# Queries and keys handed over with the head dimensions first: the on-chip transposes and copies ahead of the feature projection go away

## The chip, the core and the metric

The kernel runs on one core of a Trainium2 chip. The metric is device time in microseconds (us), from launch to the last output in memory; how the host arranges its arrays before the launch is not in it. Five engines work side by side, each through its own instructions in order: TensorE (PE: matrix products and transposes; its weight loads have their own row, PEld), VectorE (DVE), ScalarE (ACT), GpSimd (POOL) and SyncE (SP, which here only issues DMAs). Products land in PSUM, everything else lies in SBUF.

## What is computed

Three stages follow each other, for 4 batches of 576 tokens with 8 heads of 64 dimensions (2304 tokens of 512 features). Cut to what matters:

```python
def phi(x):                                   # (b, h, s, 64) -> (b, h, s, 256)
    proj = einsum('bhsd,df->bhsf', x, w_phi)  # 64 -> 128 features
    proj = proj - max(abs(proj), axis=-1)
    return concatenate([exp(proj), exp(-proj)])
q_p, k_p = phi(q), phi(k)
kv = einsum('bhsf,bhsd->bhfd', k_p, v);  z = sum(k_p, axis=2)
x = (q_p @ kv) / (q_p . z + 1e-6)             # linear attention
# experts: each token goes to its best of 8 (512 -> 1024 relu -> 512), scaled by two gates
# last: RMS norm, silu(xn @ w_gate) * (xn @ w_val) @ w_out, 512 -> 1536 -> 512
```

## The kernel before

**Staging.** Attention, gating and experts of all four batches come first, planned together; the last stage comes after a branch (lines 978 and 979) that all engines reach. Attention of batch b (`attn`, line 376) goes over nine groups of [128 tokens x 4 chunks x 2 heads]: four pairs of heads of k over the first 512 tokens, one group "L" with the 64 left-over tokens of all heads (k and q together), four pairs of q.

**One group.** `load` brings 256 KB into a `qk` tile (4 of them), tokens on the partitions. `proj` (line 411) then needs the 64 head dimensions on the partitions, since a product sums over them: four 128x128 transposes on PE into a PSUM bank `pa` (line 418), one ACT copy to an SBUF tile `x0` (line 421), eight products with `w_phi` (line 428; each stands as two records in the trace) into a double bank `pp` (named pq in the trace), the largest magnitude on DVE (432), and the subtraction on DVE (434), which frees `pp`. Exponentials on ACT follow (522, 515, or 451 after transposes for q), then the products with v (492), the key sums (478 to 501), the transposes of kv (539), and for q the products 589, the division (459 to 463), transposes, and the halves of `xh`, the experts' input (600, 602).

**Experts.** The experts of batch b (lines 737 and 746, twelve 128x288 products per task) need all of its `xh`. They have a lower priority than attention and fill PE while the attention of later batches goes on.

**What sets the order.** `Graph` is a planner that runs while the kernel is built. It gives every task an assumed duration, starts whichever can start first on each engine, then the one of lower priority number, and so writes down a fixed order for each engine. Buffers of a tag come from slots; a task without a free slot waits. `retire` (lines 314 and 315) takes one `pp` double bank from attention after nine uses of `pp`, and one `pa` bank after a count of uses, and hands them to the experts as `ph` banks. So from the tenth projection on, there is one `pp`.

Of the kernel before, what the change touches and what calls it, by code (L numbers as in the profile page):

```python
# [13 lines left out]
ALU = mybir.AluOpType  # L14
# [3 lines left out]
B, H, S, D = 4, 8, 576, 64  # L18
FE = 128
# [10 lines left out]
class Buf:  # L30


    def __init__(self, tag, ap=None, hold=False):
        self.tag, self.ap, self.hold = tag, ap, hold
        self.writers, self.all, self.left, self.end, self.slot = [], [], 0, 0.0, None
# [189 lines left out]
def act(n, psum=True):  # L225
    return 0.15 + n / 1200.0


class K:
    def __init__(self, tc, q, k, v, w_phi, wg, wo, w1, w2, mg, mv, mo, rg, out):  # L230
        self.tc, self.nc = tc, tc.nc
        self.q, self.k, self.v, self.w_phi = q, k, v, w_phi
        self.wg, self.wo, self.w1, self.w2 = wg, wo, w1, w2
        self.mg, self.mv, self.mo = (a.bitcast(U32) for a in (mg, mv, mo))
        self.rg, self.out = rg, out
        self.g = Graph()
        self.marks = []
# [64 lines left out]
    def psum(self):  # L302


        self.banks, self.pair = ExitStack(), ExitStack()
        p = self.pool(self.banks, "ps", space=PSUM)
        one = [p.tile([P, 512], F32, name=f"ps{i}") for i in range(4)]
        two = [p.tile([P, 2, 512], F32, name="pq0"),
               self.pool(self.pair, "pq", space=PSUM).tile([P, 2, 512], F32, name="pq1")]
        self.last = two[0]  # L310
        self.g.slot("pa", one)
        self.g.slot("pp", two)
        self.g.slot("ph", [])
        self.g.retire("pp", 9, two[1], "ph", self.halve)
        self.g.retire("pa", 36, one[3], "ph", lambda: one[3:])

    def halve(self):

# [32 lines left out]
    def attn_slots(self, ctx):  # L351
        g, p = self.g, self.pool(ctx, "at", side="left")
        self.attn_consts(p)
        mk = lambda *a: self.mk(p, *a)
        mk("qk", 4, [P, 2, NC, D])
        mk("v", 3, [P, 2, NC, D])
        mk("vl", 2, [P, 2, NC, D])
        mk("x0", 2, [P, NC, P])
        mk("d", 3, [P, 2, NC, FE])
        mk("m", 3, [P, 2 * NC])  # L360
        mk("e", 2, [P, 2 * NC, 2, FE])
        mk("el", 1, [P, NC, 2, FE])
        for _, _, a in g.slots["vl"]:
            self.nc.gpsimd.memset(a, 0.0)
        self.ones = p.tile([P, 1], F32, name="ones")
        self.nc.gpsimd.memset(self.ones, 1.0)
        mk("es", 2, [P, 4, 2 * FE])
        mk("ks", 1, [P, 2 * FE])
        mk("qp", 2, [P, 2, NC, P])
        mk("qpl", 1, [P, 2, NC, P])  # L370
        mk("kv", 6, [P, 2, 2, D + 1])
        mk("x", 2, [P, NC, P])
        mk("xl", 1, [P, 4 * D])
        mk("r", 2, [P, NC])

    def attn(self, b, prio):
# [6 lines left out]
        def load(src, pr, np_):  # L383
            t = g.buf("qk")
            if pr != "L":
                g.t("SP", 0.5, lambda: nc.sync.dma_start(
                    t.ap, src[b, 2 * pr:2 * pr + 2, 0:MAIN].rearrange("h (p c) d -> p h c d", c=NC)),
                    w=[t], prio=np_, nbytes=2 * MAIN * D * 4)
                return t
            for i, m in enumerate((self.k, self.q)):  # L390
                for j in range(2):
                    g.t(eng, 0.6, lambda i=i, j=j, m=m: dma(
                        t.ap[j * 64:(j + 1) * 64, i], m[b, j::2, MAIN:S].rearrange("h t d -> t h d")),
                        w=[t], prio=-1 if b == 0 else np_, nbytes=LEFT * H * D * 2)
            return t

        def load_v(pr, np_):
# [12 lines left out]

        def proj(t, np_):

            pt, xt, m, d, pp = (g.buf(n) for n in ("pa", "x0", "m", "d", "pp"))

            def tr():
                for j in range(2):
                    for c in range(2):
                        nc.tensor.transpose(pt.ap[:, (2 * j + c) * P:(2 * j + c + 1) * P],
                                            t.ap[:, j, 2 * c:2 * c + 2].rearrange("p a d -> p (a d)"), self.ident)
            g.t("PE", 4 * 0.109, tr, r=[t], w=[pt], prio=np_)  # L420
            g.t("ACT", act(512), lambda: nc.scalar.copy(  # L421
                xt.ap.rearrange("p c t -> p (c t)"), pt.ap), r=[pt], w=[xt], prio=np_)

            def mm():
                for k in range(NC):
                    for hf in range(2):
                        r = slice(hf * 64, hf * 64 + 64)
                        nc.tensor.matmul(pp.ap[:, hf, k * FE:(k + 1) * FE], lhsT=xt.ap[r, k], rhs=self.wraw[r],  # L428
                                         start=True, stop=True)
            g.t("PE", 8 * 0.109 + 0.2, mm, r=[xt, self.cBw], w=[pp], prio=np_)  # L430
            pv = lambda: pp.ap.rearrange("p h (k f) -> p (h k) f", f=FE)
            g.t("DVE", dve(1024), lambda: nc.vector.tensor_reduce(  # L432
                out=m.ap, in_=pv(), axis=AX.X, op=ALU.max, apply_absolute_value=True), r=[pp], w=[m], prio=np_)
            g.t("DVE", dve(1024), lambda: nc.vector.tensor_tensor(  # L434
                out=d.ap.rearrange("p h k f -> p (h k) f"), in0=pv(),
                in1=m.ap.unsqueeze(2).to_broadcast([P, 2 * NC, FE]), op=ALU.subtract),
                r=[m, pp], w=[d], prio=np_)
            return d

        at = lambda j, c: (c % 2) * NC + 2 * j + c // 2  # L440

        def queries(d, j, qp, np_):

            pd = g.buf("pa")

            def tr():
                return [partial(nc.tensor.transpose, pd.ap[:, c * P:(c + 1) * P], d.ap[:, c % 2, 2 * j + c // 2],
                                self.ident) for c in range(NC)]
            g.t("PE", NC * 0.109, tr, r=[d], w=[pd], prio=np_, kind="pass", steps=NC)
            for f in range(2):  # L450
                g.t("ACT", act(512), lambda f=f: nc.scalar.activation(  # L451
                    qp.ap[:, f].rearrange("p c t -> p (c t)"), pd.ap, AF.Exp, scale=1.0 - 2.0 * f),
                    r=[pd], w=[qp], prio=np_)
            return pd
# [15 lines left out]
        def kv_part(pr, e, v, np_, pk, part, pz=None):  # L470
# [1 line left out]

            es = g.buf("es") if NC in part else None
            if es:
                ev = lambda: e.ap.rearrange("p (a k) f x -> p a k (f x)", a=2)
                sv = lambda: es.ap.rearrange("p (j b) x -> p j b x", j=2)
                ex = lambda: el.ap[:, (pr % 2) * 2 + pr // 2].rearrange("p f x -> p (f x)")
                g.t("DVE", dve(1024), lambda: nc.vector.tensor_tensor(
                    out=es.ap, in0=ev()[:, 0], in1=ev()[:, 1], op=ALU.add), r=[e], w=[es], prio=np_)
                g.t("DVE", dve(512), lambda: nc.vector.tensor_tensor(  # L480
                    out=sv()[:, :, 0], in0=sv()[:, :, 0], in1=sv()[:, :, 1], op=ALU.add), rw=[es], prio=np_)
                for j in range(2):
                    r = slice(j * 64, j * 64 + 64)
                    g.t("DVE", dve(256), lambda j=j, r=r: nc.vector.tensor_tensor(
                        out=sv()[r, j, 0], in0=sv()[r, j, 0], in1=ex()[r], op=ALU.add), r=[el], rw=[es], prio=np_)

            def fn():
                for c in part:
                    for j in range(2):
                        v_, e_ = (v.ap[:, j, c], e.ap[:, at(j, c)]) if c < NC else (  # L490
                            vl.ap[:, j, pr], el.ap[:, (pr % 2) * 2 + pr // 2])
                        nc.tensor.matmul(pk.ap[j * 64:j * 64 + 64, 0:2 * FE], lhsT=v_,
                                         rhs=e_.rearrange("p f e -> p (f e)"), start=(c == 0), stop=(c == NC))
# [13 lines left out]
        for i, pr in enumerate([0, "L", 1, 2, 3]):  # L507
# [4 lines left out]
            if pr == "L":  # L512
                el, vl, qpl = g.buf("el"), v, g.buf("qpl")
                for f in range(2):
                    g.t("ACT", act(512, False), lambda f=f, d=d: nc.scalar.activation(
                        el.ap[:, :, f].rearrange("p (h c) f -> p h c f", h=2), d.ap[:, :, 0:2], AF.Exp,
                        scale=1.0 - 2.0 * f), r=[d], w=[el], prio=np_)
                queries(d, 1, qpl, np_)
            else:
                e = g.buf("e")  # L520
                for f in range(2):
# [54 lines left out]
        for pr in range(NC):  # L576
# [3 lines left out]
            x = g.buf("x")  # L580
            for j in range(2):
                qp = g.buf("qp")
                pn = queries(d, j, qp, np_ + j)

                def nm(pn=pn, qp=qp, pr=pr, j=j):
                    for c in range(NC):
# [452 lines left out]
    return UT if u < B else B * LEFT  # L1039


def build(tc, ctx, q, k, v, w_phi, wg, wo, w1, w2, mg, mv, mo, rg, out):
    kk = K(tc, q, k, v, w_phi, wg, wo, w1, w2, mg, mv, mo, rg, out)
    nc, g = tc.nc, kk.g
    kk.consts(ctx)
    kk.psum()
# [56 lines left out]
    with tc.manual_schedule():  # L1103
# [10 lines left out]
        g.emit()  # L1114


_INS = ["q", "k", "v", "w_phi", "moe_w_gate", "moe_w_output_gate", "moe_w1", "moe_w2",
        "moe2_w_gate", "moe2_w_val", "moe2_w_out", "moe2_rms_g"]


# [19 lines left out]
```

## Time and profile before

| | us |
|---|---|
| runs, median (lowest to highest) | 871.34 (870.13 to 871.94) |
| the profiled execution | 868.49 |
| its span, first to last instruction | 866.9 |
| PE busy in the span | 853.7 |
| DVE busy | 468.3 |
| ACT busy | 326.4 |
| four transposes per group, 36 groups, PE busy (line 418) | 21.1 |
| copies of line 421, ACT busy | 20.8 |

A busy time of PE is the sum of modelled stretches that overlap; a better price of a group of products is the distance from its first start to the first start of the next group, as the timeline gives it. The granted clock of PE is 0.999 of its full level over the span.

### The profile page before, as it was taken

The numbers are of one execution on the slowest core, as the hardware profiler recorded it, in microseconds if no ns is written. First come the engines' busy times: TensorE is split into PE (matmuls) and PEld (weight loads), VectorE is DVE, ScalarE is ACT, GpSimd is POOL, SyncE is SP. The second block draws the span as 40 slices with busy tenths as digits, with TensorE's granted clock in tenths as the row PEclk, the third lists the DMA queues.
The fourth block names the chain that finished last, engine by engine and source line by source line (L and its number), as shares of the span: only waits on it lengthen the run. The fifth ranks groups of instructions, "written<-read, shape, count | busy, mean of one in ns | idle before, by whom it ended". The sixth has DMA issues, their size and how long they took to land.

```text
span 866.9 us, 15321 instructions
## 1 busy us (share of the span) xinstructions
PE 853.7 (98%) x6482; PEld 738.1 (85%) x6483; DVE 468.3 (54%) x866; ACT 326.4 (38%) x559; POOL 2.8 (0%) x17
## 2 busy tenths in 40 slices
PE   8999999999999999999999999999999999999997
PEld 6778998899889999998888889988788888888886
DVE  6987775776776489992757842431414114221111
ACT  5474453535544365550535533221214112221111
POOL 1000000000000000000000000000000000000000
PEclk9999999999999999999999999999999999999999
DMA  7354316420611656851524420020002000010001
GB/s 196 97 159 165 104 34 209 128 86 26 218 29 40 223 172 186 260 169 58 168 75 125 143 98 1 11 63 1 0 1 98 0 1 1 1 48 1 1 1 48
DMA packets 71914, 74.63 MB, mean 86 GB/s; under 512 B 13600, under 2 KB 63392, under 8 KB 71328
## 3 DMA queue, kind: packets, MB, share of 16 engines
q1 hardware_dynamic: 70592, 73.27, 26.9%
q8 instruction: 52, 0.85, 0.4%
q10 hardware_dynamic: 1248, 0.33, 0.2%
q14 instruction: 22, 0.18, 0.1%
HBM read 54.63 MB, written 18.96 MB: 85 GB/s over the span
## 4 chain that ended last, share of the span: by engine, by line
PE 52%; DVE 0%; ACT 0%; issue 0%
PE pz L925 35%; PE pz L943 17%; PE pz L896 0%; DVE yu L955 0%; ACT yu L958 0%
## 5 line engine op out<-in xcount | busy, mean ns | idle before, releaser
L925 PE MATMUL pz<-xn,wgv 128*128 128x512 f32 (+1 forms) x1200 | 258.2, 371 | 2.1 <-PEq L979 2.1
L925 PEld LDWEIGHTS pz<-xn,wgv 128*128 128x128 f32 x1200 | 210.2, 188 | 43.9 <-issue 2.3
L943 PE MATMUL pz<-wo,a 128*128 128x512 f32 x648 | 159.7, 394 | 0.0
L933 DVE TENSOR_TENSOR row<-pz,row 128x512 f32<-128x512 f32 (+1 forms) x60 | 38.2, 636 | 203.8 <-PE pz L925 200.2
L943 PEld LDWEIGHTS pz<-wo,a 128*128 128x128 f32 x648 | 121.0, 188 | 28.2 <-issue 1.4
L931 ACT ACTIVATE row<-pz 128x512 f32<-128x512 f32 (+1 forms) x60 | 33.3, 555 | 154.8 <-PE pz L925 154.6
L935 ACT CAST a<-row 128x512 fp32r<-128x512 f32 (+1 forms) x60 | 34.6, 577 | 120.5 <-DVE row L933 120.5
L737 PE MATMUL ph<-xh,w 128*128 128x288 f32 x528 | 77.6, 298 | 0.0
L737 PEld LDWEIGHTS ph<-xh,w 128*128 128x128 f32 x528 | 71.4, 188 | 0.4
L746 PE MATMUL ph<-h,w 128*128 128x288 f32 x480 | 69.5, 298 | 0.0
L746 PEld LDWEIGHTS ph<-h,w 128*128 128x128 f32 x480 | 64.7, 188 | 0.2
L432 DVE TENSOR_REDUCE m<-pq 128x8 f32<-128x1024 f32 x36 | 43.8, 1218 | 16.5 <-PE pq L428 16.5
L925 PE MATMUL pz<-xn,xh 128*128 128x512 f32 (+1 forms) x240 | 52.3, 373 | 0.0
L936 DVE TENSOR_TENSOR a<-row,a 128x512 fp32r<-128x512 f32 (+1 forms) x60 | 38.2, 637 | 25.8 <-ACT a L935 25.6
L925 PEld LDWEIGHTS pz<-xn,xh 128*128 128x128 f32 x240 | 42.1, 188 | 8.9
L767 ACT CAST w<-wr 128x1024 fp32r<-128x1024 f32 x32 | 33.5, 1048 | 31.0 <-PE ph L746 11.2
L428 PE MATMUL pq<-wraw,x 64*128 64x128 f32 x576 | 41.4, 284 | 2.9 <-DVE d L434 2.0
L768 DVE TENSOR_TENSOR w<-wr,w 128x1024 fp32r<-128x1024 f32 x32 | 39.1, 1221 | 9.6 <-ACT w L767 8.8
L434 DVE TENSOR_TENSOR d<-pq,m 128x1024 f32<-128x1024 f32 x36 | 43.7, 1217 | 0.4
L451 ACT ACTIVATE qp<-ps 128x512 f32<-128x512 f32 x64 | 34.4, 600 | 21.4 <-PE ps L210 17.6
L746 PE MATMUL ps<-h,w 128*128 128x288 f32 x288 | 41.9, 297 | 0.0
L428 PEld LDWEIGHTS pq<-wraw,x 64*128 64x128 f32 x576 | 34.9, 187 | 7.7 <-ACT x L421 2.9
(151 smaller groups left out, 934.4 us busy)
## 6 DMA issues: line engine op xcount, KB each, us to landing
wr<-in_moe_w SPq DMA_DIRECT2D x32, 512.0 KB, 4.3
xdr<-xh SPq DMA_DIRECT2D x4, 2304.0 KB, 9.0
raw<-in_moe_w_gate SPq DMA_DIRECT2D x12, 512.0 KB, 4.4
raw<-in_moe_w_val SPq DMA_DIRECT2D x12, 512.0 KB, 4.4
raw<-in_moe_w_out SPq DMA_DIRECT2D x12, 512.0 KB, 3.7
qk<-in_k SPq DMA_DIRECT2D x16, 256.0 KB, 3.4
v<-in_v SPq DMA_DIRECT2D x16, 256.0 KB, 2.8
qk<-in_q SPq DMA_DIRECT2D x16, 256.0 KB, 3.9
```

The lines of the kernel that those rows point to most:

```text
L428: nc.tensor.matmul(pp.ap[:, hf, k * FE:(k + 1) * FE], lhsT=xt.ap[r, k], rhs=self.wraw[r], start=True, stop=True)
L432: g.t("DVE", dve(1024), lambda: nc.vector.tensor_reduce(out=m.ap, in_=pv(), axis=AX.X, op=ALU.max, apply_absolute_value=True), r=[pp], w=[ ...
L434: g.t("DVE", dve(1024), lambda: nc.vector.tensor_tensor(out=d.ap.rearrange("p h k f -> p (h k) f"), in0=pv(), in1=m.ap.unsqueeze(2).to_bro ...
L451: g.t("ACT", act(512), lambda f=f: nc.scalar.activation(qp.ap[:, f].rearrange("p c t -> p (c t)"), pd.ap, AF.Exp, scale=1.0 - 2.0 * f), r= ...
L737: self.nc.tensor.matmul(ph[:, 0:HS], lhsT=wv[:, a, c, fs], rhs=xh[:, x, c, cs], start=(c == 0 and i == 0), stop=(c == NC - 1 and i == 2))
L746: self.nc.tensor.matmul(ph[:, 0:HS], lhsT=wv[:, a, f], rhs=hs[f][:, x, cs], start=(f == 0 and i == 0), stop=(f == 7 and i == 2))
L768: g.t("DVE", dve(1024), lambda: nc.vector.tensor_tensor(out=w.ap[:, 1], in0=wr.ap, in1=w.ap[:, 0], op=ALU.subtract), r=[wr], rw=[w], prio= ...
L925: nc.tensor.matmul(ps.ap[:, 0:UT], lhsT=w[:, i, a, c], rhs=xn[c].ap[:, x, 0:UT], start=(c == 0 and n == 0), stop=(c == NC - 1 and n == 2))
L933: g.t("DVE", dve(UT), lambda sil=sil, ps=pgv[1]: nc.vector.tensor_tensor(out=sil.ap[:, 0:UT], in0=ps.ap[:, 0:UT], in1=sil.ap[:, 0:UT], op= ...
L935: g.t("ACT", act(UT, False), lambda sil=sil, a=a: nc.scalar.copy(a.ap[:, 0, 0:UT], sil.ap[:, 0:UT]), r=[sil], w=[a], prio=pr)
L936: g.t("DVE", dve(UT), lambda sil=sil, a=a: nc.vector.tensor_tensor(out=a.ap[:, 1, 0:UT], in0=sil.ap[:, 0:UT], in1=a.ap[:, 0, 0:UT], op=ALU ...
L943: nc.tensor.matmul(po[t].ap, lhsT=a.ap[:, x, ts], rhs=w[:, y], start=(f == 0 and n == 0), stop=(f == NF - 1 and n == 2))
```

## The change

Arrays for k and q are arranged on the host as [batch, pair, 128, 512]: the partition is head-in-pair times 64 plus head dimension, the columns are four chunks of 128 tokens. The left-overs of k and q come as a new input `l`, [batch, 128, 512]. A `qk` tile, six of them now, is itself the operand of the products. Transposes, copies, the `x0` tiles and the `pa` bank that a projection took are gone. The left-overs of a batch are one DMA and not four. Chunks now belong to one head, so the indices of `d` and `e` in later steps change, with the same shapes. The count after which attention gives up its `pa` bank goes from 36 to 22, as fewer uses of `pa` are made.

```diff
         self.g.retire("pp", 9, two[1], "ph", self.halve)
-        self.g.retire("pa", 36, one[3], "ph", lambda: one[3:])
+        self.g.retire("pa", 22, one[3], "ph", lambda: one[3:])
...
-        mk("qk", 4, [P, 2, NC, D])
+        mk("qk", 6, [P, NC, P])
...
-        mk("x0", 2, [P, NC, P])
...
             if pr != "L":
-                g.t("SP", 0.5, lambda: nc.sync.dma_start(
-                    t.ap, src[b, 2 * pr:2 * pr + 2, 0:MAIN].rearrange("h (p c) d -> p h c d", c=NC)),
+                g.t("SP", 0.5, lambda: nc.sync.dma_start(t.ap, src[b, pr].rearrange("p (c t) -> p c t", c=NC)),
                     w=[t], prio=np_, nbytes=2 * MAIN * D * 4)
-                return t
-            for i, m in enumerate((self.k, self.q)):
-                for j in range(2):
-                    g.t(eng, 0.6, lambda i=i, j=j, m=m: dma(
-                        t.ap[j * 64:(j + 1) * 64, i], m[b, j::2, MAIN:S].rearrange("h t d -> t h d")),
-                        w=[t], prio=-1 if b == 0 else np_, nbytes=LEFT * H * D * 2)
+            else:
+                g.t(eng, 0.6, lambda: dma(t.ap, self.l[b].rearrange("p (c t) -> p c t", c=NC)),
+                    w=[t], prio=-1 if b == 0 else np_, nbytes=2 * MAIN * D * 4)
             return t
...
-            pt, xt, m, d, pp = (g.buf(n) for n in ("pa", "x0", "m", "d", "pp"))
-
-            def tr():
-                for j in range(2):
-                    for c in range(2):
-                        nc.tensor.transpose(pt.ap[:, (2 * j + c) * P:(2 * j + c + 1) * P],
-                                            t.ap[:, j, 2 * c:2 * c + 2].rearrange("p a d -> p (a d)"), self.ident)
-            g.t("PE", 4 * 0.109, tr, r=[t], w=[pt], prio=np_)
-            g.t("ACT", act(512), lambda: nc.scalar.copy(
-                xt.ap.rearrange("p c t -> p (c t)"), pt.ap), r=[pt], w=[xt], prio=np_)
+            m, d, pp = (g.buf(n) for n in ("m", "d", "pp"))
...
-                        nc.tensor.matmul(pp.ap[:, hf, k * FE:(k + 1) * FE], lhsT=xt.ap[r, k], rhs=self.wraw[r],
+                        nc.tensor.matmul(pp.ap[:, hf, k * FE:(k + 1) * FE], lhsT=t.ap[r, k], rhs=self.wraw[r],
                                          start=True, stop=True)
-            g.t("PE", 8 * 0.109 + 0.2, mm, r=[xt, self.cBw], w=[pp], prio=np_)
+            g.t("PE", 8 * 0.109 + 0.2, mm, r=[t, self.cBw], w=[pp], prio=np_)
...
                 g.t("DVE", dve(1024), lambda: nc.vector.tensor_tensor(
-                    out=es.ap, in0=ev()[:, 0], in1=ev()[:, 1], op=ALU.add), r=[e], w=[es], prio=np_)
+                    out=sv(), in0=ev()[:, 0], in1=ev()[:, 1], op=ALU.add), r=[e], w=[es], prio=np_)
...
+    for n in "qk":
+        a = inputs[n][:, :, :MAIN].reshape(B, NC, 2, P, NC, D)
+        lay[n] = a.transpose(0, 1, 2, 5, 4, 3).reshape(B, NC, P, MAIN)
+    a = np.stack([inputs[n][:, :, MAIN:].reshape(B, 2, 2, 2, LEFT, D) for n in "kq"])
+    lay["l"] = a.transpose(1, 3, 6, 0, 2, 4, 5).reshape(B, P, MAIN)
```

The planner then writes other orders. PE at the start of the program, before; the first row is a run of products that only warm the engine, and qk_150 and qk_151 are the first two pairs of k:

```order
L334 MATMUL ps_81<-mean 128x128 x8
L418 MATMUL ps_82<-ident,qk_150 128x128 x4
L418 MATMUL ps_83<-ident,qk_151 128x128 x4
L428 MATMUL pq_85<-wraw,x_0_159 128x128 x8
L428 MATMUL pq_89<-wraw,x_1_160 128x128 x8
L418 MATMUL ps_84<-ident,qk_153 128x128 x4
```

The same place now (line 414 is the projection that was line 428, line 476 was 492):

```order
L334 MATMUL ps_81<-mean 128x128 x8
L414 MATMUL pq_85<-wraw,qk_150 128x128 x8
L414 MATMUL pq_89<-wraw,qk_151 128x128 x8
L414 MATMUL pq_85<-wraw,qk_152 128x128 x8
L414 MATMUL pq_89<-wraw,qk_153 128x128 x8
L476 MATMUL ps_82<-e_167,v_156 64x256 x8
```

The projections moved up to right behind the warming run; nothing of ACT stands between the load and them.

PE where the experts of batch 0 begin, before (line 737 is the first expert task, the rows of line 418 belong to batch 1, and x_187 is the last pair of batch 0):

```order
L418 MATMUL ps_83<-ident,qk_152 128x128 x4
L418 MATMUL ps_83<-ident,qk_150 128x128 x4
L418 MATMUL ps_84<-ident,qk_151 128x128 x4
L418 MATMUL ps_83<-ident,qk_153 128x128 x4
L428 MATMUL pq_85<-wraw,x_0_159 128x128 x8
L210 MATMUL ps_81<-ident,x_187 128x128 x4
L492 MATMUL ps_82<-el_169,vl_158 64x256 x2
L210 MATMUL ps_84<-ident,d_162 128x128 x4
L418 MATMUL ps_81<-ident,qk_152 128x128 x4
L737 MATMUL ph_578<-xh_93,w_119 128x288 x12
```

The same place now, up to the gate's products (lines 632 to 638, formerly 648 to 654), which the first expert task follows:

```order
L210 MATMUL ps_84<-ident,x_186 128x128 x4
L476 MATMUL ps_83<-el_169,vl_160 64x256 x2
L210 MATMUL ps_81<-ident,d_162 128x128 x4
L485 MATMUL ps_83<-ones,es_174 64x1 x8
L414 MATMUL pq_85<-wraw,qk_155 128x128 x8
L523 MATMUL ps_83<-ident,ks_176 128x128 x2
L210 MATMUL ps_82<-ident,x_187 128x128 x4
L632 MATMUL ps_81<-xh_93,wgt 32x288
```

Up to its first expert task PE had 64 of the 144 transposes of line 418 and 96 of the 288 products of line 428; the products are again 96 now. The gate's sixteen products, one set of key sums and one pair of kv transposes moved ahead of the first expert task.

ACT at the start of the program, before:

```order
L299 DMA wraw<-in_w_phi 64x128 x2
L392 DMA qk_152<-in_k 64x4x64 x2
L392 DMA qk_152<-in_q 64x4x64 x2
L256 ACT_TABLE_LOAD
L256 ACTIVATE one<-eps 128x1
L421 COPY x_0_159<-ps_82 128x512
L421 COPY x_1_160<-ps_83 128x512
```

ACT at the same place now:

```order
L299 DMA wraw<-in_w_phi 64x128 x2
L388 DMA qk_152<-in_l 128x512
L256 ACT_TABLE_LOAD
L256 ACTIVATE one<-eps 128x1
L506 ACTIVATE e_167<-d_161 128x8x128 x2
```

Three of the four left-over loads and the copies are gone there; the table load stays ahead of the first exponential.

## Rows read from the trace of the kernel before

**Rows 1.** Page, busy time of each engine, and shares of the last chain:

```profile
PE 853.7 (98%) x6482; PEld 738.1 (85%) x6483; DVE 468.3 (54%) x866; ACT 326.4 (38%) x559; POOL 2.8 (0%) x17
...
PE pz L925 35%; PE pz L943 17%; PE pz L896 0%; DVE yu L955 0%; ACT yu L958 0%
```

**Rows 2.** Busy time by stretch: length, engines (instructions), clock, DMA share, GB/s:

```profile
0.00:8.00 8.00, 5.79 (x44) 5.57 (x47) 0.01 (x1) 2.46 (x5) 2.77 (x17) 1.00 0.66 179
8.00:63.00 55.00, 51.17 (x752) 41.28 (x750) 51.65 (x93) 33.30 (x55) 0.00 (x0) 1.00 0.48 137
63.00:292.00 229.00, 228.77 (x2741) 204.69 (x2740) 164.42 (x352) 107.98 (x193) 0.00 (x0) 1.00 0.33 106
292.00:409.00 117.00, 114.70 (x858) 112.61 (x856) 88.77 (x164) 55.11 (x95) 0.00 (x0) 1.00 0.61 189
409.00:867.00 458.00, 453.23 (x2096) 373.95 (x2096) 163.49 (x257) 127.55 (x211) 0.00 (x0) 1.00 0.13 42
```

**Rows 3.** Waits from 0 to 64 us, PE's, then DVE's (total, times, longest):

```profile
PE pq L428 <- DVE d L434: 2.0, 2, 1.6
PE ps L418 <- ACT x L421: 0.9, 2, 0.7
...
DVE m L432 <- PE pq L428: 8.1, 2, 7.9
DVE es L484 <- ACT el L515: 0.9, 1, 0.9
DVE xh L602 <- ACT xh L600: 0.8, 1, 0.8
```

**Rows 4.** PE's waits from 64 to 409 us (the whole answer):

```profile
PE ps L737 <- DVE h L786: 0.5, 1, 0.5
```

**Rows 5.** Timeline, the program's first microseconds (start, us, what):

```profile
4.81 1.28 ACT L256 ACT_TABLE_LOAD   x1 [4.68 <-DMA wraw<-in_w_phi]
4.87 1.04 PE L418 MATMUL ps<-ident,qk 128*128 128x128 f32 x8
...
6.21 1.05 ACT L421 COPY x<-ps 128x512 f32<-128x512 f32 x2
...
6.83 2.06 PE L428 MATMUL pq<-wraw,x 64*128 64x128 f32 x32 [0.92 <-ACT x L421]
...
8.04 2.35 DVE L432 TENSOR_REDUCE m<-pq 128x8 f32<-128x1024 f32 x2 [7.93 <-PE pq L428]
```

**Rows 6.** Timeline of PE from 142.8 to 152 us:

```profile
142.87 0.60 PE L418 MATMUL ps<-ident,qk 128*128 128x128 f32 x4
143.40 1.16 PE L428 MATMUL pq<-wraw,x 64*128 64x128 f32 x16
...
147.77 0.60 PE L418 MATMUL ps<-ident,qk 128*128 128x128 f32 x4
148.13 1.85 PE L746 MATMUL ph<-h,w 128*128 128x288 f32 x12
149.81 1.04 PE L418 MATMUL ps<-ident,qk 128*128 128x128 f32 x8
150.60 1.84 PE L746 MATMUL ph<-h,w 128*128 128x288 f32 x12
```

**Rows 7.** Busy time of line 418's instructions alone, by stretch (PE, then PEld):

```profile
0.00:63.40 63.40, 8.61 (x60) 6.57 (x60) 1.00 0.51 144
63.40:292.00 228.60, 12.50 (x84) 9.30 (x84) 1.00 0.33 105
```

**Rows 8.** Timeline of PE from 63 to 68 us:

```profile
63.83 1.84 PE L737 MATMUL ph<-xh,w 128*128 128x288 f32 x12
65.60 0.63 PE L501 MATMUL ps<-ones,es 128*64 128x1 f32 x16
66.16 1.16 PE L428 MATMUL pq<-wraw,x 64*128 64x128 f32 x16
67.26 0.44 PE L539 MATMUL ps<-ident,ks 128*128 128x128 f32 x2
67.45 0.78 PE L737 MATMUL ph<-xh,w 128*128 128x288 f32 x4
```

## What the change will do, predicted before it ran

> **What bounds the kernel now.** I read the page's engines and last chain first [rows 1]: PE is busy 98% of the span, and the chain that ended last is PE alone in the last stage (lines 925 and 943). The change touches nothing there, so the next view is the busy time by stretch [rows 2]. It shows four regimes. Up to 8 us DVE does nothing: the first projection has not come. From 8 to 63 us DVE is busy 51.65 of 55 us and PE 51.17: the attention of batch 0 runs alone, with both nearly full. From 63 to 292 us PE is busy 228.77 of 229 us and DVE 164.42: the experts of batch 0 have begun (first task at 63.83 us [rows 8]) and fill whatever attention leaves. From 292 to 409 us PE works off the remaining expert tasks, 114.70 of 117 us, DVE 88.77. The last stage takes 458 us.
>
> The waits say the same. From 64 to 409 us PE waited for another engine once, 0.5 us [rows 4]; up to 64 us there are several waits, and most of DVE's is the 7.9 us before its first instruction [rows 3]. So the program is: a lead-in that ends when the last half of `xh` of batch 0 is there, then a pile of PE work that is done without a pause, then the last stage. Time can be won by a shorter lead-in or a smaller pile. The granted clock reads 1.00 in every stretch, so durations need no correction.
>
> **Part 1, the start of the lead-in.** Before, the first eight transposes start at 4.87 us, the copies on ACT at 6.21 (behind the table load of 1.28 us that began at 4.81), the projection at 6.83, and DVE's first instruction at 8.04 [rows 5]. Now the projections stand right behind the warming run. Both loads had landed when the eight transposes ran, since these ran on without a gap, and `w_phi` had landed at 4.68, as the wait ahead of the table load tells. So the projection can start where the transposes did: 6.83 - 4.87 = **1.96 us** earlier, and DVE with it. The table load, which was a cover for nothing, now lies beside PE and DVE work; the first exponential needs it only after DVE's two passes, more than 2 us later [rows 5].
>
> **Part 2, the rest of the lead-in.** DVE's work up to the last `xh` of batch 0 is almost the same set of instructions, so it can only lose its idle time, which is 55 - 51.65 = 3.35 us between 8 and 63 us [rows 2]. What ended these waits was ACT in 0.9 and 0.8 us cases [rows 3], and PE waited 0.9 us for the copies themselves; 14 of the 36 copies stand there on ACT. Ends: 0 and 3.35 us. I take half, **1.7 us**: ACT's queue gets shorter, but the transposes of the results, the exponentials and the divisions stay a chain of their own.
>
> **Part 3, the pile on PE.** 84 of the 144 transposes run after 63.4 us [rows 7], 21 groups of four; the 60 before lie in the lead-in and are counted there. Price of a group by first starts [rows 6]: ahead of an expert task 148.13 - 147.77 = 0.36 us; eight in a row 150.60 - 149.81 = 0.79, or 0.40 for four; ahead of a projection 143.40 - 142.87 = 0.53. Ends: 21 x 0.36 = 7.6 us and 21 x 0.53 = 11.1 us. Most groups stand ahead of expert tasks, alone or in pairs, so I take 0.41 x 21 = **8.6 us**. Their busy time, 12.50 us [rows 7], is no price, as the modelled ends overlap.
>
> **Part 4, work that moved ahead.** One set of key sums and one pair of kv transposes now stand before the first expert task: 66.16 - 65.60 = 0.56 and 67.45 - 67.26 = 0.19, together **0.75 us** off the pile [rows 8]. In the lead-in PE has lost 60 transposes, so there is room for them. The gate's sixteen products also moved ahead, but behind the last `xh`, where PE has to do them anyway: nothing.
>
> **Part 5, what costs nothing.** 22 copies on ACT in the pile's stretch: ACT is busy 107.98 of 229 us there [rows 2], so their end frees nobody. The DMAs carry as many bytes, in longer runs, and the left-overs in one transfer and not four; the loads' share of the engines is 0.33 of the pile's stretch [rows 2], and no wait of PE there is on a load [rows 4]. The queues are SP's, and ACT's for batch 0: SP is relieved of twelve issues, and ACT of three ahead of its table load. A `qk` tile is now held until its projection has run, not only until its transposes have; the two more tiles are the cover, and without it a load would wait for a projection. The key sum in line 478 reads and writes the same number of elements. The earlier exit of one `pa` bank (22 uses) matches what projections no longer take.
>
> **Where the gain could stop.** When PE's pile ends sooner, DVE is next: between 292 and 409 us it is idle for 117 - 88.77 = 28 us [rows 2], more than the sum below. If attention ended later than PE's savings suggest, 28 us of slack would still hide it.
>
> **The sum.** 1.96 + 1.7 + 8.6 + 0.75 = 13.0 us. The profiled execution took 868.49 us, of which 866.9 is the span and 1.6 lies around it; that makes 855.5. It lay 2.85 us under the median of the runs, 871.34; on the median's scale the forecast is **858.3 us**.
>
> **Rival A, PE has room.** The transposes could lie in room that PE has anyway. For it: PEld is busy only 204.69 of 229 us in the pile's stretch, so 24 us are not held by weight loads [rows 2]. Against it: no wait is named there [rows 4], and the starts of a group and of its successor lie as far apart as the group's own work [rows 6]. If it held, parts 3 and 4 would give nothing, and 1.96 + 1.7 = 3.7 us would remain: 871.34 - 3.7 = 867.6 us. The Trainium skill (Perfetto Trace Analysis, Identifying the Most-Contended Engine) says that matmul busy time misleads and that the busy share of weight loads tells how far PE is from its limit; by that rule the pile's stretch has a tenth to spare and rival A's time would be the one to expect. The trace agrees only in that the two shares differ; the single wait speaks for a PE that is full with short products whose weights load fast.
>
> **Rival B, the lead-in keeps its length.** The copies and transposes could be replaced by other waits in the lead-in, since the orders of DVE and PE there are new and both engines are nearly full. Then parts 1 and 2 give nothing, and 8.6 + 0.75 = 9.4 us remain: 862.0 us. For it: DVE's wait for ACT is partly for the division's chain, which stays [rows 3]. Against it: the first 1.96 us come before any of that.
>
> **Rival C, the projection waits for its bank.** Slower. The place: from the tenth projection on there is one `pp`, which DVE's subtraction frees. Before, PE had transposes to do in this time; now a projection can stand in PE's order right where the planner thinks the bank is free, and everything behind it waits, expert tasks included. The price: before, such a wait came twice, 2.0 us together, so 1.0 us each [rows 3]. With 24 projections after the lead-in (288 - 96 products, eight each), all waiting so long, it is 24 us against 13.0: 871.34 + 11 = 882.3 us. It decides from 13.0 / 24 = 0.54 us per projection; below about 0.47 the kernel is faster beyond what can be told, above 0.61 slower. Against it: after 64 us no projection waited [rows 4], and DVE is busy 164.42 of 229 us there, so it is seldom late. A few such waits, 2 us in all, belong to my range.
>
> **How the numbers follow.** About 0.2%, or 1.7 us, is what a measurement of this kernel can tell from no change. Forecast with its bounds 0.78; rival A 0.06; rival B 0.10; rival C 0.06, of which the middle part, where waits and savings cancel, is 0.02. Faster: 0.78 + 0.06 + 0.10 = 0.94, less 0.01 for a rival A in which the lead-in gains too little; same 0.03; slower 0.04. Lower end: 1.96 + 3.35 + 11.1 + 0.75 = 17.2, or 854.1 us. Upper end of the forecast: 1.96 + 0 + 7.6 + 0, less 2.0 of new waits, is 7.6, or 863.8 us; rival B lies within. Range 854 to 864.5.
>
> **What would show it.** In the profile after: DVE's first instruction near 6.1 us; the first expert task, or the gate's products ahead of it, near 60 us; line 418's and 421's groups gone; the last stage beginning near 396 us and again 458 us long; PE's waits between there still under 2 us. Rival A would show as new idle time of PE without a changed end of the pile, rival C as PE's projection waiting for DVE's subtraction. I am wrong if the last stage itself changes its length, or if the pile shrinks by much less than its transposes.

## The result and the profile after

The changed kernel takes **859.16 us** (median; 856.76 to 860.32), the kernel before in the same comparison 870.74 us (869.95 to 871.94): 0.9862 of it, 95% interval 0.9837 to 0.9887. Forecast were 858.3 us and a range of 854 to 864.5. The profiled execution took 859.16 us with a span of 857.5, 9.3 us less than the one of before.

The page of the changed kernel, busy time of each engine and the shares of its last chain; they answer to [rows 1]:

```profile
PE 843.1 (98%) x6338; PEld 726.5 (85%) x6339; DVE 468.3 (55%) x866; ACT 306.9 (36%) x523; POOL 2.8 (0%) x17
...
PE pz L909 35%; PE pz L927 17%; PE pz L880 0%; DVE yu L939 0%; ACT yu L942 0%
```

PE lost 144 instructions and 10.6 us of busy time, ACT 36 and 19.5; DVE's work is the same. PE is still the end of everything.

The busy time of the changed kernel by stretch, with the columns of [rows 2], cut where its regimes lie:

```profile
0.00:8.00 8.00, 6.70 (x48) 6.49 (x49) 0.64 (x2) 1.50 (x3) 2.78 (x17) 1.00 0.75 203
8.00:63.00 55.00, 49.33 (x713) 39.27 (x710) 50.82 (x95) 28.93 (x46) 0.00 (x0) 0.94 0.46 131
63.00:283.00 220.00, 219.59 (x2633) 194.00 (x2633) 164.54 (x350) 94.13 (x169) 0.00 (x0) 1.00 0.34 111
283.00:400.00 117.00, 114.26 (x856) 112.88 (x854) 88.49 (x164) 54.94 (x94) 0.00 (x0) 1.00 0.59 189
400.00:867.00 467.00, 453.25 (x2096) 373.89 (x2096) 163.80 (x257) 127.40 (x211) 0.00 (x0) 1.00 0.13 41
```

The window of the last row runs on to 867 us, past the end of the span at 857.5. The pile is shorter by the 9 us that separate 292 from 283; the work of the two stretches behind it is the same as before (PE 114.26 and 453.25 us, before 114.70 and 453.23). The lead-in is not shorter, and one column says what is new in it: the granted clock is 0.94 there, and was 1.00.

The timeline of the changed kernel, first its start, then the last half of batch 0's `xh`, then the first product of the last stage (start, us, what); it answers to [rows 5]:

```profile
5.01 3.22 PE L414 MATMUL pq<-wraw,qk 64*128 64x128 f32 x32
...
7.38 2.36 DVE L418 TENSOR_REDUCE m<-pq 128x8 f32<-128x1024 f32 x2 [7.26 <-PE pq L414]
...
10.92 3.48 PE L414 MATMUL pq<-wraw,qk 64*128 64x128 f32 x32 [2.69 <-DVE d L420]
...
62.67 0.69 DVE L586 TENSOR_TENSOR xh<-ps,xh 128x512 fp32r<-128x512 f32 x1 [0.36 <-ACT xh L584]
...
400.24 4.12 PE L909 MATMUL pz<-xn,wgv 128*128 128x512 f32 x17 [2.31 <-PEq L963]
```

The same two marks in the kernel before:

```profile
62.67 0.69 DVE L602 TENSOR_TENSOR xh<-ps,xh 128x512 fp32r<-128x512 f32 x1
409.30 2.06 PE L925 MATMUL pz<-xn,wgv 128*128 128x512 f32 x8 [2.09 <-PEq L979]
```

The first projections start at 5.01 us instead of 6.83, but 32 records of them take 3.22 us and not 2.06. The last half of `xh` starts at 62.67 us, exactly as before, and ends at 63.36. From there to the last stage it is 400.24 - 63.36 = 336.9 us, where it was 409.30 - 63.36 = 345.9: nearly the whole gain of this execution, 9.06 of 9.3 us, lies in the pile.

PE's waits in the changed kernel, from 0 to 64 us and then from 64 to 400 us (total, times, longest), against [rows 3, 4]:

```profile
PE pq L414 <- DVE d L420: 3.5, 3, 2.7
...
PE ph L721 <- DVE h L770: 0.7, 1, 0.7
```

In the lead-in a projection now waits for DVE's subtraction; the longest of these waits, 2.69 us ahead of 10.92, has no transposes of PE's in it any more. In the pile there is one wait of 0.7 us, where there was one of 0.5.

The granted clock of the changed kernel in the lead-in (behind the stretch a row has its length, PE's busy time with the number of records, the clock, the DMA share and GB/s):

```profile
8.00:12.00 4.00, 1.31 (x14) 0.82 1.09 308
12.00:16.00 4.00, 4.00 (x42) 0.76 0.67 186
16.00:30.00 14.00, 12.67 (x151) 1.00 0.46 113
30.00:34.00 4.00, 2.60 (x34) 1.00 0.48 148
34.00:38.00 4.00, 4.00 (x38) 0.57 0.00 0
```

From 8 to 12 us PE was busy 1.31 of 4 us, and the clock of that and the next stretch is 0.82 and 0.76, a mixture of both levels (2.4 and 1.2 GHz); from 30 to 34 us it was busy 2.60 of 4, and then the clock is 0.57: 16 records of a projection, 1.16 us elsewhere, take 2.08 us at 35.48. Ahead of about 7 us the record gives no level, and the row's 1.00 means nothing; the 3.22 us do.

### The profile page after: what moved, and what is told of

Its sections match the earlier page's. It is cut to its first block, busy times and chain, and to the rows that moved or that the text cites. A ratio compares the mean times of both kernels' runs of the same rounds, so it can differ in the third digit from the quotient of the medians.

```text
span 857.5 us, 14956 instructions
## 1 busy us (share of the span) xinstructions
PE 843.1 (98%) x6338; PEld 726.5 (85%) x6339; DVE 468.3 (55%) x866; ACT 306.9 (36%) x523; POOL 2.8 (0%) x17
## 3 DMA queue, kind: packets, MB, share of 16 engines
HBM read 54.63 MB, written 18.96 MB: 86 GB/s over the span
## 4 chain that ended last, share of the span: by engine, by line
PE 53%; DVE 0%; ACT 0%; issue 0%
PE pz L909 35%; PE pz L927 17%; PE pz L880 0%; DVE yu L939 0%; ACT yu L942 0%
## 5 line engine op out<-in xcount | busy, mean ns | idle before, releaser
L414 PE MATMUL pq<-wraw,qk 64*128 64x128 f32 x576 | 44.8, 299 | 3.5 <-DVE d L420 3.5
L414 PEld LDWEIGHTS pq<-wraw,qk 64*128 64x128 f32 x576 | 38.2, 202 | 8.6 <-DVE d L420 4.4
```

The source lines that it names most:

```text
L414: nc.tensor.matmul(pp.ap[:, hf, k * FE:(k + 1) * FE], lhsT=t.ap[r, k], rhs=self.wraw[r], start=True, stop=True)
```

## The experiments

Two theories stood against each other on the lead-in, and one on the pile. **P**: the pile lost its transposes, and the lead-in lost what it had saved to the clock. **D**: the lead-in is as long as the chain of DVE and ACT, whatever the clock. **R**: PE has room in the pile and the transposes had cost little. Marks of all profiles, in us, from the starts and ends of instructions in that kernel's timeline:

| kernel | DVE's first | last `xh` starts | between these | last stage starts | pile | last stage lasts | median of runs |
|---|---|---|---|---|---|---|---|
| before | 8.04 | 62.67 | 54.63 | 409.30 | 345.9 | 457.6 | 870.3 to 870.7 |
| changed | 7.38 | 62.67 | 55.29 | 400.24 | 336.9 | 457.3 | 859.16 |
| again | 7.97 | 62.31 | 54.34 | 399.71 | 336.7 | 457.6 | 858.91 |
| again_b | 6.60 | 59.72 | 53.12 | 397.17 | 336.8 | 458.8 | 859.38 |
| fill | 6.09 | 59.10 | 53.01 | 396.49 | 336.7 | 458.9 | 856.97 |
| fill_b | 6.38 | 59.39 | 53.01 | 396.76 | 336.7 | 458.9 | 857.06 |
| fill2 | 7.00 | 60.01 | 53.01 | 400.72 | 340.0 | 458.7 | 860.82 |
| pile_tr | 6.00 | 63.57 | 57.57 | 412.34 | 348.1 | 457.8 | 872.04 |
| act_copy | 7.14 | 63.91 | 56.77 | 399.75 | 335.1 | 458.9 | 859.73 |
| old_lead | 8.18 | 62.48 | 54.30 | 400.02 | 336.9 | 459.2 | 861.43 |
| old_pile | 6.71 | 60.12 | 53.41 | 408.44 | 347.6 | 459.4 | 870.17 |
| qk4 | 6.74 | 59.78 | 53.04 | 397.45 | 337.0 | 458.9 | 857.75 |
| pa36 | 6.54 | 60.88 | 54.34 | 397.26 | 335.7 | 458.9 | 858.45 |

"Pile" is from the end of the last `xh` to the first product of the last stage; in "fill2" it holds ten more products and a longer wait behind them.

### The same kernel again (again, again_b)

No edit.

> The changed kernel once more, nothing altered; it is the measure for the others of this group. Theory P (the pile of PE work behind the lead-in became shorter by its transposes, and the lead-in gained nothing because PE's granted clock fell to half twice in it): about 859 us again, and the end of the lead-in (last subtraction of batch 0's xh, 62.67 us in the first profile) moves with the places of the half-clock stretches. Theory D (the lead-in is as long as DVE's and ACT's chain makes it, whatever PE's clock): about 859 us, and that end stays at 62.7 within 0.3 us.

> The changed kernel once more, beside both: 859 within 1 us. Theory P: its lead-in ends between 59 and 63 us, the later the more half-clock time its record shows before 62 us; theory D: at 62.5 within 0.3 us.

Measured: 858.91 us (858.69 to 858.93) and 859.38 us (857.64 to 860.43). Timelines, the first products and the last `xh`, of "again":

```profile
5.01 4.63 PE L414 MATMUL pq<-wraw,qk 64*128 64x128 f32 x32
...
62.31 0.69 DVE L586 TENSOR_TENSOR xh<-ps,xh 128x512 fp32r<-128x512 f32 x1 [0.32 <-ACT xh L584]
```

and of "again_b":

```profile
5.41 2.05 PE L414 MATMUL pq<-wraw,qk 64*128 64x128 f32 x30
...
59.72 0.69 DVE L586 TENSOR_TENSOR xh<-ps,xh 128x512 fp32r<-128x512 f32 x1 [0.36 <-ACT xh L584]
```

The clock's stretches of "again_b", columns as above:

```profile
8.00:12.00 4.00, 1.86 (x22) 0.91 1.06 316
12.00:16.00 4.00, 4.00 (x32) 0.66 0.61 208
16.00:30.00 14.00, 13.04 (x160) 1.00 0.47 116
30.00:34.00 4.00, 3.01 (x42) 1.00 0.40 98
34.00:38.00 4.00, 4.00 (x112) 1.00 0.20 70
```

The same instructions in the same order come to the last `xh` at 59.72, 62.31 or 62.67 us. In "again_b" the first 30 records take 2.05 us and there is one low stretch near 12 us; in the first profile there are two, and a slow start; in "again" the record shows the full level only from 17 us on, and the first 32 records take 4.63 us (0.35 of it waiting for `w_phi`). Theory D, which wanted 62.5 within 0.3 us, falls. The three differ in DVE's start too (6.60, 7.97 and 7.38 us), so not all of the 3 us is lost behind it: from DVE's first instruction to the last `xh` they take 53.12, 54.34 and 55.29 us.

### Keeping PE at work in the lead-in (fill, fill_b)

```diff
+    def fill(self, n, at):
+        w = self.g.buf("pa")
+        for i in range(n):
+            self.g.t("PE", 0.214, lambda: self.nc.tensor.matmul(
+                w.ap[:, 0:P], lhsT=self.mean, rhs=self.mean, start=True, stop=True), rw=[w], prio=3000, at=at)
...
+FILL = ((12, 7.3), (4, 29.95), (3, 31.65))
...
         kk.warm(8)
+        for n, at in FILL:
+            kk.fill(n, at)
```

The count after which attention gives up its bank rose by three, for the three banks taken here. DVE, ACT and SP have the same orders as in the changed kernel.

> 19 products of the warming kind (128x128 with the matrix of means, result unused) are put where PE waits in the lead-in: 12 between the second and the third projection, 4 and 3 around the key sums near 31 us; all other instructions keep their order. Theory P: no half-clock stretch after the first rise of the clock, the lead-in ends 2 to 3 us earlier, near 60 us, and the time falls by 1.5 to 3 us against the changed kernel, to 856 to 857.5. Theory D: the clock stays up, the lead-in ends at 62.7 as before, 859 us. If the fillers get in the way: 860 to 861.

> The kernel with fillers in the lead-in alone, again, beside the one with fillers in both places: 857 within 0.7 us.

Measured: 856.97 us (856.06 to 857.18), 0.9849 of before [0.9829, 0.9869], and 857.06 us (856.37 to 857.75), 0.9852 [0.9834, 0.9871], beside 858.91 and 859.38 us for the changed kernel in the same comparisons: about 2 us less, and the two lowest medians of all. The timeline of "fill", with the fillers as line 341:

```profile
4.71 2.23 PE L421 MATMUL pq<-wraw,qk 64*128 64x128 f32 x32
6.09 2.36 DVE L425 TENSOR_REDUCE m<-pq 128x8 f32<-128x1024 f32 x2 [5.98 <-PE pq L421]
...
6.88 2.94 PE L341 MATMUL ps<-mean 128*128 128x128 f32 x24
...
59.10 0.69 DVE L593 TENSOR_TENSOR xh<-ps,xh 128x512 fp32r<-128x512 f32 x1 [0.36 <-ACT xh L591]
```

and its clock:

```profile
8.00:12.00 4.00, 4.00 (x51) 1.00 1.06 294
12.00:16.00 4.00, 3.29 (x36) 1.00 0.80 244
16.00:30.00 14.00, 12.99 (x151) 1.00 0.44 102
30.00:34.00 4.00, 4.00 (x62) 1.00 0.31 90
34.00:38.00 4.00, 4.00 (x108) 1.00 0.25 66
```

The clock is at its full level throughout the lead-in; the last `xh` starts at 59.10 and 59.39 us, 3.3 to 3.6 us earlier than in the kernel before. Work that nobody reads made the program faster, so the lead-in depends on PE's clock and not on DVE's and ACT's chain alone.

Not all of the 3.3 to 3.6 us comes from the fillers. The first of them starts at 6.88 us, behind the products that set DVE's start of 6.09, so they can't have brought that about. What they can change is the time from DVE's first instruction to the last `xh`: 53.01 us in all three profiles with fillers ("fill2" too), 53.12 to 55.29 in the three of the changed kernel, so 0.1 to 2.3 us less and 1.2 on average. Whether the rest of the 2 us in the medians is theirs, or that of starts that differ from run to run, is open.

### Transposes put back into the pile (pile_tr)

```diff
             def mm():
+                for k in range(NC if b > 0 else 0):
+                    nc.tensor.transpose(pp.ap[:, 0, k * P:(k + 1) * P], t.ap[:, k], self.ident)
                 for k in range(NC):
```

> The changed kernel, but each projection of batches 1 to 3 has four 128x128 transposes ahead of its products again (into the bank that the products then overwrite; no copy on ACT, nobody reads them). 24 of the 27 groups lie behind the first expert task. Theory P and D (PE is full in the pile): 24 x 0.36 to 24 x 0.53, so 8.6 to 12.7 us more than the changed kernel, about 869.5. Theory R (PE has room in the pile, as the 85% busy share of its weight loads suggests): within 2 us of the changed kernel, 859 to 861.

Measured: 872.04 us (870.91 to 874.13). PE's timeline of this kernel around 102 us:

```profile
101.39 0.63 PE L487 MATMUL ps<-ones,es 128*64 128x1 f32 x16
101.95 0.66 PE L412 MATMUL pq<-ident,qk 128*128 128x128 f32 x4
102.54 1.16 PE L416 MATMUL pq<-wraw,qk 64*128 64x128 f32 x16
```

By first starts a group in front of a projection costs 102.54 - 101.95 = 0.59 us here. The pile is 348.1 us, 11.4 more than in "again", or 0.47 for each of 24 groups, inside the expected 0.36 to 0.53. Summed by first starts over this trace, the 24 groups come to 13.2 us (0.53 to 0.59 each), so that price was 1.8 us too high here. Theory R falls. The total is 13.1 us above "again", over the expected 8.6 to 12.7: this profile's last `xh` starts at 63.57, with three of the extra groups ahead of it and a clock of 0.66 from 30 to 40 us.

### The copies on ACT put back (act_copy)

```diff
-        mk("qk", 6, [P, NC, P])
+        mk("qk", 4, [P, NC, P])
+        mk("x0", 2, [P, NC, P])
...
+            g.t("ACT", act(512), lambda: nc.scalar.copy(xt.ap, t.ap), r=[t], w=[xt], prio=np_)
...
-                        nc.tensor.matmul(pp.ap[:, hf, k * FE:(k + 1) * FE], lhsT=t.ap[r, k], rhs=self.wraw[r],
+                        nc.tensor.matmul(pp.ap[:, hf, k * FE:(k + 1) * FE], lhsT=xt.ap[r, k], rhs=self.wraw[r],
```

> The changed kernel, but each projection reads a copy that ACT makes of the loaded tile (two tiles for the copies, four for the loads, as before); no transposes. It brings the ACT half of the removed work back by itself. Theory P and D: ACT is off the path in the pile, so only the start can move, by the copy of 0.59 us and its handing over, 0.6 to 2 us: 859.8 to 861. If the copies on ACT had held PE back in the pile: 863 or more.

Measured: 859.73 us (857.29 to 860.32), within 1 us of the changed kernel. 36 copies on ACT, waits included, are worth nothing that can be told in the time. In the profile the last `xh` comes 1.2 us later than in the first profile of the changed kernel and the pile is 1.7 us shorter. So what the change gained in the pile it gained on PE; whether copies or transposes made the lead-in's part is not told apart.

### One half of the change at a time (old_lead, old_pile)

The core of the edit is one condition, which chooses between the old load, transposes, copy and chunk order and the new ones; four `qk` and two `x0` tiles serve both, and the bank leaves after 31 (old_lead) and 27 uses (old_pile). Shortened, with comments added:

```diff
+        old = b == 0          # old_lead; old_pile has b > 0
...
+            xt = t
+            if old:
+                pt, xt = g.buf("pa"), g.buf("x0")
+                ...           # four transposes into pt, copy to xt
```

> Batch 0 loads, transposes and copies as before the change; batches 1 to 3 as after it. Theory P: the lead-in is the one of before, 62.7 us with the clock up after the first rise, the pile the one of after, 336.8 us: 859.5 to 861.5, so next to nothing is lost against the changed kernel, because its own lead-in loses to the clock what it saves. If the new lead-in is worth its 3.6 us in most runs: 862.5 or more.

> Batch 0 as after the change, batches 1 to 3 with loads, transposes and copies as before it. Theory P: pile near 346 us, lead-in between 59.1 us (clock up throughout) and 62.7 us (half-clock stretches): 867 to 870.5. Theory R (PE has room in the pile): 859 to 861.

Measured: old_lead 861.43 us (859.03 to 862.17), 0.9894 of before [0.9865, 0.9922]; old_pile 870.17 us (867.42 to 873.01), 0.9999 [0.9983, 1.0015]. With the old lead-in and the new pile, 9 us of the gain are there (pile 336.9); the time came out as expected, though the clock was not up in this profile (0.75 and 0.50 from 34 to 38 us). With the new lead-in and the old pile nothing remains of it: in the profile the last `xh` starts 2.5 us earlier, but the pile is 1.7 and the last stage 1.8 us longer than before. By old_lead the pile's share of the 11.6 us is about 9 and the lead-in's about 2, so in the median the new lead-in did gain something, other than theory P had it; old_pile shows the pile's share, but no gain from the new lead-in alone.

### Two settings that came with the change (qk4, pa36)

```diff
-        mk("qk", 6, [P, NC, P])
+        mk("qk", 4, [P, NC, P])
```

```diff
-        self.g.retire("pa", 22, one[3], "ph", lambda: one[3:])
+        self.g.retire("pa", 36, one[3], "ph", lambda: one[3:])
```

> The changed kernel with four qk tiles instead of six. The prediction called the two more tiles the cover of loads that are now held until their projection has run. If so, loads start later and PE waits for them or for what follows: 1 to 4 us more, 860 to 863. If four are enough, since a projection comes soon after its load: 859 within 1 us.

> The changed kernel with the count of 36 uses kept, after which attention gives up its fourth pa bank: it does so later, and the experts have two banks for longer. Theory P (PE is full in the pile either way): within 1 us of 859. If the third expert bank is what keeps PE full early in the pile: 1 to 3 us more, and waits of expert tasks for DVE or ACT.

Measured: 857.75 us (857.41 to 858.83) and 858.45 us (857.80 to 859.82). Neither is slower; "qk4" lies 1.4 us under the expected 859, and "pa36" within 1 us of it. Four tiles are enough, and the bank's exit may be late.

### Fillers ahead of the last stage (fill2)

```diff
+LAST = (10, 391.7)
...
         kk.yB = yB
+        kk.fill(*LAST)
         g.emit()
```

> The kernel with fillers in the lead-in, and ten more products of the warming kind behind the last expert task, where PE otherwise idles for 2.1 to 2.5 us ahead of the last stage's branch. If that idle time is what lets the clock fall at the start of the last stage (458.9 us instead of 457.4 in several profiles): the last stage takes 457.4 us in every profile and the time falls by 0.5 to 1.5 us against the fillers alone, to 855.5 to 856.5. If the branch waits for the fillers: the last stage begins 1 to 2 us later and the time is 858 to 859.

Measured: 860.82 us (860.46 to 861.10). PE's timeline at the branch:

```profile
395.10 2.39 PE L341 MATMUL ps<-mean 128*128 128x128 f32 x20
...
400.72 3.47 PE L916 MATMUL pz<-xn,wgv 128*128 128x512 f32 x8 [3.22 <-PEq L970]
```

and the clock behind it:

```profile
400.00:404.00 4.00, 3.28 (x8) 0.57 0.58 195
404.00:410.00 6.00, 6.00 (x28) 1.00 0.58 187
```

This is above both expectations. The branch waits until the fillers are done, and then PE stands still for 3.22 us more, longer than without them (2.14 in "fill"); the clock falls all the same. What sets the length of this gap was not found.

## Why the prediction was right, and where it was not

**What bounds the kernel** held in its large parts: a lead-in, a pile without pauses, an untouched last stage (457.3 us against 457.6 in the two profiles).

**Parts 3 and 4, the pile**, were summed at 8.6 + 0.75 = 9.35 us; it became 409.30 - 400.24 = 9.06 us shorter, as the last `xh` ended at 63.36 us in both profiles. Taking the distance of first starts as the price, and not the busy time of 12.50 us [rows 7], was what made this fit: over all 21 groups of the trace before, these distances come to 8.5 us, so the 0.41 read off a few of them was no lucky choice. Putting the transposes back cost 0.47 us a group, between the two ends.

**Part 1** put DVE's start 1.96 us earlier. In "fill" it is 8.04 - 6.09 = 1.95 us, in the first profile of the changed kernel 0.66, in "again" 0.07. With projections at the start, DVE begins anywhere from 6.00 us ("pile_tr", which has no fillers) to 7.97; with fillers it is 6.09, 6.38 and 7.00. Two things differed from run to run. The record first shows the full clock at about 4.4 us in "fill", 7.1 in the first profile and 17 in "again". And PE's weight loads waited for `w_phi` in three profiles, 0.35, 0.34 and 0.79 us ("again", "again_b", "fill2"). The prediction let `w_phi` land at 4.68 us; that number is the length of ACT's idle time, which ended when its table load began at 4.81, so the margin ahead of 4.87 was small.

**Part 2** put 1.7 us on the rest of the lead-in. From DVE's first instruction to the last `xh` it is 54.63 us before and 53.01 in each profile with fillers, so 1.62 less. In "again_b" and "qk4", whose clock fell once, near 12 and near 24 us, it is 53.12 and 53.04; in "pa36", where it fell near 35 us, 54.34; in the first profile, with falls near 12 and 36 us, 55.29, so there the 0.66 us of gain at the start were gone at the end. The size was right, but only where no costly fall of the clock took it away.

**The step that failed** is a sentence on what bounds the kernel: "The granted clock reads 1.00 in every stretch, so durations need no correction." It took the clock of one execution for that of the kernel. That execution lay 2.85 us under the median, and the other runs of the kernel before show a lower clock with a longer time: of the seventeen beside "again", those with a mean granted clock of 0.999 or 1.000 took 868.35 to 869.00 us, those with 0.995 or 0.996 took 871.29 to 871.92. In the three profiles of the changed kernel the clock fell in the lead-in at other places each time, or rose late, and the 3.7 us of parts 1 and 2 came out as 0, 0.4 and 2.9 us; with fillers they were 2.7 to 3.6. In the median of runs the whole is 11.6 us, where 13.0 were forecast. That 858.3 and 859.16 us lie closer together than 13.0 and 11.6 is luck of the base: the forecast started from 871.34, but beside the result the kernel before took 870.74, and from there the sum gives 857.7.

That the old transposes had held the clock up in these waits is not shown. The profile before has no fall in its lead-in, but "old_lead", with the same transposes there, has one near 36 us, and where the slower runs of the kernel before lost their time is not on record.

**Rival B** gave 862.0 us, and for the first profile its outcome was exact: parts 1 and 2 gave nothing, and 9.3 us of its 9.4 remained. But it put the loss on other waits of DVE and PE. The wait of 2.69 us for the bank is there in "qk4" too, which came to its last `xh` 2.9 us earlier; with fillers the clock stayed up and 2 us came back. **Rival A** fell with pile_tr. The Trainium skill (Perfetto Trace Analysis, Identifying the Most-Contended Engine) names the busy share of weight loads as one of two measures of PE's room. Here this share is 194.00 of 220 us in the pile, and 96 transposes nevertheless cost 11.4 us, so the starts of successive groups were the better judge. **Rival C** had its place right and its stretch wrong: projections did wait for DVE's subtraction, 3.5 us in three times, but in the lead-in and not in the pile.

**Part 5** was wrong on one point: the two more `qk` tiles are no cover that the kernel needs. SP is relieved of nine issues and not of twelve (three stay), which changes nothing in the sum. That ACT's copies and the bank's exit cost nothing in the pile was right. That the loads cost nothing rests on the waits of PE; no run changed the loads alone.

## What to carry to other kernels

Price a group of PE work by the distance from its start to that of the next one, in the stretch where PE never waits. There, what was removed came back in full (8.5 us by first starts and 0.75 us that moved ahead, 9.3 together, against 9.06 measured); put back ahead of projections it cost 11.4 us where first starts say 13.2. In a stretch where PE does wait, do not take the clock of one profile for that of the kernel: look at the clock of the other runs first. Where it falls, some products of no use in the wait are a cheap test, and here also a cure of 2 us in the medians.

## What the runs showed of the hardware

The granted clock fell inside a running program and came back by itself. In the first profile of the changed kernel it fell after stretches in which PE was busy 1.31 and 2.60 of 4 us. But the same wait for the bank does not always bring a fall. In "pile_tr", "qk4" and "pa36" a projection near 10 us waited 2.69 to 2.70 us, PE was busy 2.46, 1.72 and 1.92 of 4 us from 8 to 12 us, and the clock stayed up to 16 us; the rows of "pile_tr":

```profile
8.00:12.00 4.00, 2.46 (x34) 1.00 1.02 317
12.00:16.00 4.00, 3.42 (x38) 1.00 0.75 245
```

Where the clock falls seems to matter as well. With one fall near 12 or 24 us ("again_b", "qk4") it was 53.12 and 53.04 us from DVE's first instruction to the last `xh`, hardly more than the 53.01 with fillers and no fall; with one near 35 us ("pa36") it was 1.3 us more. One profile of each is too few to price a fall.

The Trainium skill (TensorE: Matmul & The Clock Gate, HAM oscillation) describes a kernel whose PE slows down again after each wait for its loads. These traces agree in part: here the waits were for a bank (at 10.9 us) and at the last stage's branch, where the clock of "fill2" read 0.57 from 400 to 404 us, and not every such wait brought a fall. Where it fell at the branch, the last stage took 458.7 to 459.4 us instead of 457.3 to 457.8. That stood in nine of the thirteen profiles, and a gap of 2.31 us at the branch brought a fall in "old_lead" and none in the first profile of the changed kernel; why was not settled.
